# Attention on one Trainium2 core: products with V in groups of 3, 3, 3, 3, 2, 2 key tiles, a fixed order of one head, PSUM banks chosen by a count, nine P tiles, gate columns summed earlier

## The chip, the cores and the metric

The kernel runs on one core of one Trainium2 chip. The metric is the time of one execution on the device in microseconds (us). The engines of the core are named as the profile names them: PE (TensorE, with PEld for its weight loads), DVE (VectorE), ACT (ScalarE), POOL (GpSimd) and SP (SyncE, which issues DMAs). Each engine takes its instructions in program order. A difference of 0.2% is about what a measurement of this kernel can tell from none.

## The reference

A block with two halves, both gated by a condition vector `c`: attention with 16 heads of width 28 over 2048 rows of 448, and a gated MLP that mixes over rows. What the change touches is the first half and the six modulation vectors:

```
mod = (_silu(c) @ w_mod).reshape(c.shape[0], 6, 1, -1)
sa, ca, ga, sb, cb, gb = (mod[:, 0], mod[:, 1], mod[:, 2], mod[:, 3], mod[:, 4], mod[:, 5])
h = _layernorm(x, axis=-1) * (1 + ca) + sa
x = x + ga * _A_ref(h, A_wqkv, A_wo)
h = _layernorm(x, axis=-1) * (1 + cb) + sb
x = x + gb * _B_ref(h, B_w_in, B_w_sp, B_b_sp, B_w_out)
```

`_A_ref` is softmax attention: `q k^T / sqrt(28)`, softmax over the keys, times `v`, times `wo`. All of it is in float32.

## The kernel before

Every order is written out by hand: each engine runs its instructions as the program lists them, and an instruction waits only for the data or the buffer that it needs.

The attention stage runs head by head, in units `u` of one head and one tile of 128 keys (16 units a head, 256 in all). Unit `u` has four score products (`s_mm`, L649, out `st_ps`: 128 keys by 512 queries), each followed by an exponential on ACT (L653) into a P tile; and one product with V (`pv_mm`, L664, out `o_ps`), which is four matmuls on 32-column strips of the array, one for each block of 512 queries. These accumulate over the 16 key tiles of a head in one PSUM bank. The softmax needs a row maximum ahead of it. So the kernel also computes, 20 units earlier (`LEAD`), the transposed scores (`m_mm`, L584, out `mt`), and DVE reduces each to a column of maxima (L589, out `pm`). A head therefore has 64 score products, 64 products for the maxima and 16 products with V. At the end of a head's maxima, `m_max` (three short DVE steps, `mxv` and `mx`) and `m_fin` (a transpose on PE into `mtp`, a copy on DVE into `nf`, two DMAs from `nf` into two rows of `qst`) put the maxima where the next head's score products subtract them. `nf` is a single buffer. `n_copy` (L673, out `osb`) takes a finished `o_ps` off PSUM, and `n_sum`, `n_recip`, `n_bcast`, `n_mul` and `n_scatter` divide it by the sum of its P.

The order of the steady loop: unit after unit, `s m s m s m s m`, and behind every second unit the products with V of the two units before it, a group of 2 key tiles. PSUM has eight banks: three in turn for the scores (tag `s`), four in turn for the maxima (tag `m`), one for `o_ps`. A product into a bank waits until the reader of the bank's last content is done. P tiles (one holds 128 by 1024) come from a pool of six, which is three units.

All other work hangs on the units as events: loads of the next head, 80 sums of weight blocks for the second half (`ws_load`, `ws_add` on POOL, `ws_store`), and the gates. `mod_late` multiplies a tile of `w_late` by the silu row on POOL and sums it in halves into a column; `mod_end` adds one or turns the column into a row (`to_row`: a transpose into `mtp`, a copy into the same `nf`, a DMA from it). Sixteen of them are spread 10 units apart, in the order ga, sb, cb, gb. `wo_prep` scales and splits the output weight by `ga` at units 124 to 148, and `wout_prep` the last weight by `gb` at units 199 to 235.

Of the kernel before, what the change touches and what calls it, by code (L numbers as in the profile page):

```python
# [8 lines left out]
F32 = mybir.dt.float32  # L9
F32R = mybir.dt.float32r  # L10
AF = mybir.ActivationFunctionType
ALU = mybir.AluOpType
# [21 lines left out]
def tile_adaln_mha_gmlp(ctx, tc, x, wqkv, wo, w_in, w_spT, b_sp, w_out, cT, w_mod, w_late, out):  # L34
# [129 lines left out]
    def bank(name, kind=None):  # L164

        if kind is None:
            kind = "smsmsmm"[turn[0] % 7]
            turn[0] += 1
        return ring.tile([128, 512], F32, name=name, tag=kind, bufs=3 if kind == "s" else 4)

    def load_mod_chunk(c, eng):
# [390 lines left out]


    ppool = att.enter_context(tc.tile_pool(name="ppool", bufs=6))

    class Slots:

# [4 lines left out]
            return heapD[n][p, o : o + c.stop - c.start]  # L572

    OT = Slots()
    wos = hview(heapD[2], 0, 8, D)

    pms = {}

    steady = []

    def m_mm(j, kb):
        h, t = divmod(j, NT)
        mt = bank("mt", *steady)
        pe.matmul(  # L584
            mt, qst[h % 3][:, t * 128 : (t + 1) * 128], kst[h % 3][:, kb * 512 : (kb + 1) * 512], start=True, stop=True
        )
        if h not in pms:
            pms[h] = npool.tile([128, NT, 4], F32, name="pm")
        dve.tensor_reduce(out=pms[h][:, t, kb : kb + 1], in_=mt, axis=AX.X, op=ALU.max)  # L589

    mxs = {}

    def m_max(h):
        nm = npool.tile([128, NT], F32, name="mxv")
        dve.tensor_reduce(out=nm, in_=pms.pop(h), axis=AX.X, op=ALU.max, negate=True)
        mxs[h] = npool.tile([128, 2 * NT], F32R, name="mx2")
        dve.tensor_copy(mxs[h][:, 0:NT], nm)
        sub(dve, mxs[h][:, NT : 2 * NT], nm, mxs[h][:, 0:NT])

    def m_fin(h):  # L600
        mx = mxs.pop(h)
        tp = bank("mtp", *steady)
        pe.transpose(tp[0 : 2 * NT, 0:128], mx.bitcast(F32), ident)
# [5 lines left out]
    LATE = ("ga", "sb", "cb", "gb")  # L609
    gcols = {"sb": cols["sb"], "cb": cols["cb"], "ga": cols["sa"], "gb": cols["ca"]}  # L610
    mods = {}

    def silu_row():
        sp.dma_start(bcs["gb"], row(0))

    def mod_load(i):
        mods[i] = stage2.tile([128, D], F32, name="w_late", tag="ql")
# [2 lines left out]
    def mod_late(i):  # L620
        m, n = mods.pop(i), D // 2

        def add(dst, a, b):
            pool.tensor_tensor(out=dst, in0=a, in1=b, op=ALU.add)

        pool.tensor_tensor(out=m, in0=m, in1=bcs["gb"], op=ALU.mult)
        while n >= 7:
            add(m[:, 0:n], m[:, 0:n], m[:, n : 2 * n])
            n //= 2
        add(m[:, 0:3], m[:, 0:3], m[:, 3:6])  # L630
        add(m[:, 0:1], m[:, 0:1], m[:, 1:2])
        add(m[:, 2:3], m[:, 2:3], m[:, 6:7])
        add(gcols[LATE[i // 4]][:, i % 4 : i % 4 + 1], m[:, 0:1], m[:, 2:3])

    def mod_end(nm):
        if nm == "cb":
            pool.tensor_scalar(out=cols[nm], in0=cols[nm], scalar1=1.0, scalar2=None, op0=ALU.add)
        elif nm != "sb":
            to_row(gcols[nm], 1, *steady)

    def mod_row(nm):
        sp.dma_start(bcs[nm], row(1))
# [2 lines left out]

    def s_mm(u, qb):
        h, kt = divmod(u, NT)
        st = bank("st_ps", "s" if u + LEAD < NU else None)
        pe.matmul(st, kst[h % 3][:, kt * 128 : (kt + 1) * 128], qst[h % 3][:, qb * 512 : (qb + 1) * 512], start=True, stop=True)  # L649
# [3 lines left out]
        act.activation(p, st, AF.Exp, scale=SCALE)  # L653
        ptiles[u, qb] = p
# [2 lines left out]
    osb = {}  # L657

    def pv_mm(u):
        h, kt = divmod(u, NT)  # L660
        if kt == 0:
            otile[h] = ps_o.tile([128, 512], F32, name="o_ps", tag="o")
        for qb in range(4):
            pe.matmul(  # L664
                otile[h][32 * qb : 32 * qb + 32, :], V[:, kt, h, :], ptiles.pop((u, qb)), start=kt == 0, stop=kt == NT - 1
            )

    rts = {}

    def n_copy(h):  # L670
        osb[h] = stage.tile([128, 512], F32, name="osb", tag="qf")
        if h < H - 1:
            dve.tensor_copy(osb[h], otile.pop(h))  # L673
        else:
            act.activation(osb[h], otile.pop(h), AF.Copy)
# [55 lines left out]

    def wo_prep(i):
        pool.tensor_tensor(out=wo_raw[i], in0=wo_raw[i], in1=bcs["ga"], op=ALU.mult)
        weight_part(wos, i, wo_raw.pop(i), pool, pool)

    wout_t = {}

# [58 lines left out]

    LEAD = 20
    NU = H * NT
    events, late = {}, {}

    def at(slot, fn, *a, when=events):
# [2 lines left out]
    for h in range(H):  # L804
        if h >= 2:
            at(h * NT - LEAD - 10, load_head, h)
        e0 = (h + 1) * NT
        at(e0 + 1, n_copy, h)
# [5 lines left out]
        at(h * NT + NT - LEAD, m_max, h)  # L814
        at(max(h * NT + NT - LEAD, -2), m_fin, h, when=late)
    for c, hl in ((0, 4), (1, 9), (2, 13)):
        for qb in range(4):
            at((hl + 1) * NT + (12 + qb if c == 2 else 18 + 2 * qb), o_split, c, qb)
# [3 lines left out]
        at(slot + 5, ws_store, i)  # L822
    at(4, silu_row)
    for i in range(16):
        at(8 + 10 * i, mod_load, i)
        at(12 + 10 * i, mod_late, i)
    for i, nm in enumerate(LATE):
        at(46 + 40 * i, mod_end, nm, when=late)
        if nm in bcs:
            at(49 + 40 * i, mod_row, nm)  # L830
    for i in range(4):
        at(120 + 8 * i, wo_load, i)
        at(124 + 8 * i, wo_prep, i)
        at(200 + 8 * i, win_first, i)
    for f in range(7):
        at(196 + 6 * f, wout_raw, f)
        at(199 + 6 * f, wout_prep, f)
        at(201 + 6 * f, wout_store, f)

    load_head(1)  # L840

# [20 lines left out]
    steady.append("m")  # L862
    for u in range(NU + 1):
        for fn, a in events.pop(u, []):
            fn(*a)
        j = u + LEAD
        for qb in range(4 if u < NU else 0):
            s_mm(u, qb)
            if j < NU:
                m_mm(j, qb)  # L870
        if u % 2 == 0 and u > 0:
            pv_mm(u - 2)
            pv_mm(u - 1)
        for fn, a in late.pop(u, []):
            fn(*a)
    tail_events = {fn.__name__: [(fn, a)] for k in sorted(events) for fn, a in events[k]}

    def run_tail(*names):
# [5 lines left out]


    att.close()

    fh = ctx.enter_context(tc.tile_pool(name="fh", bufs=1))
    heapA = fh.tile([128, 8 * 896], F32R, name="heapA")
# [12 lines left out]
    def wo_mm(t, steps):  # L902
        if t not in wo_ps:
            wo_ps[t] = bank("wo_ps") if t % 8 < 7 else ps_o.tile([128, 512], F32, name="wo_ps", tag="o")
        for a, b in steps:
            pe.matmul(  # L906
                wo_ps[t][:, :D],
                OT[:, a, t * 128 : (t + 1) * 128],
                wos[:, b, :],
                start=(a, b) == STEPS[0],  # L910
                stop=(a, b) == STEPS[-1],
            )
# [539 lines left out]
```

## Time and profile before

| | |
|---|---|
| median of 3 runs | 1398.41 us (1398.05 to 1398.46) |
| the profiled execution | 1399.65 us |
| its span, first to last instruction | 1397.8 us |
| granted TensorE clock in it | 1.000 |
| DVE busy in the span | 1012.1 us (72%) |
| ACT busy in the span | 774.8 us (55%) |
| POOL busy in the span | 351.3 us (25%) |
| first and last score product | 147.1 and 864.0 us |

The page puts PE at 100% busy, yet matmuls are pipelined and each record lasts longer than the distance to the next one: a product of 512 columns has a record of 0.39 us, and the next begins 0.23 us after it. So PE's time is read from the starts of its matmuls, not from its busy share. For DVE and ACT the busy share can be read directly.

The attention stage takes half of the span, from 147 to 868 us. The other stages before and behind it have the same code in both kernels.

### The profile page before, as it was taken

The numbers are of one execution on the slowest core, as the hardware profiler recorded it, in microseconds if no ns is written. First come the engines' busy times: TensorE is split into PE (matmuls) and PEld (weight loads), VectorE is DVE, ScalarE is ACT, GpSimd is POOL, SyncE is SP. The second block draws the span as 40 slices with busy tenths as digits, with TensorE's granted clock in tenths as the row PEclk, the third lists the DMA queues.
The fourth block names the chain that finished last, engine by engine and source line by source line (L and its number), as shares of the span: only waits on it lengthen the run. The fifth ranks groups of instructions, "written<-read, shape, count | busy, mean of one in ns | idle before, by whom it ended". The sixth has DMA issues, their size and how long they took to land.

```text
span 1397.8 us, 20319 instructions
## 1 busy us (share of the span) xinstructions
PE 1391.5 (100%) x7187; PEld 989.6 (71%) x7187; DVE 1012.1 (72%) x1738; ACT 774.8 (55%) x1491; POOL 351.3 (25%) x452
## 2 busy tenths in 40 slices
PE   9999999999999999999999999999999999999998
PEld 8888655555555555555555555988998888888888
DVE  7588888888888888888888851750366655667473
ACT  5623677777766666767777778363234544334110
POOL 2043315332435254423221231000142430000000
PEclk9999999999999999999999999999999999999999
DMA  7364744666565556655334212434103333446353
GB/s 224 111 193 150 204 116 158 176 181 171 163 178 173 172 172 190 176 165 158 112 94 115 61 51 72 163 120 140 46 11 103 113 113 107 144 140 214 134 176 105
DMA packets 104406, 194.59 MB, mean 139 GB/s; under 512 B 17302, under 2 KB 34718, under 8 KB 101758
## 3 DMA queue, kind: packets, MB, share of 16 engines
q1 hardware_dynamic: 101874, 189.45, 44.7%
q10 hardware_dynamic: 2430, 3.84, 0.7%
q8 instruction: 56, 0.92, 0.3%
q14 instruction: 46, 0.38, 0.1%
HBM read 134.78 MB, written 53.67 MB: 135 GB/s over the span
## 4 chain that ended last, share of the span: by engine, by line
PE 98%; DVE 1%; ACT 0%; issue 0%; POOL 0%; POOLq 0%
PE st_ps L649 18%; PE o_ps L664 17%; PE mt L584 17%; PE acc L1224 6%; PE acc L1225 6%; PE acc L1226 6%; PE z_ps L1150 5%; PE z_ps L1036 5%; PE pq L288 5%; PE wo_ps L906 3%; PE pv L273 2%; PE y_ps L1326 2%; PE y_ps L1325 2%; PE y_ps L1327 2%; PE tp L118 1%; PE wu L237 1%
## 5 line engine op out<-in xcount | busy, mean ns | idle before, releaser
L589 DVE TENSOR_REDUCE pm<-mt 128x1 f32<-128x512 f32 x1024 | 631.1, 680 | 82.6 <-PE mt L584 82.2
L653 ACT ACTIVATE P<-st_ps 128x512 f32<-128x512 f32 x1024 | 514.6, 632 | 205.6 <-PE st_ps L649 205.6
L649 PE MATMUL st_ps<-qst,kst 128*128 128x512 f32 x1024 | 404.3, 406 | 0.2 <-DVE qf L294 0.2
L584 PE MATMUL mt<-kst,qst 128*128 128x512 f32 x1024 | 403.4, 394 | 0.1
L649 PEld LDWEIGHTS st_ps<-qst,kst 128*128 128x128 f32 x1024 | 191.3, 188 | 136.0 <-issue 92.2
L664 PE MATMUL o_ps<-P,V 128*32 128x512 f32 x2048 | 247.1, 598 | 0.0
L584 PEld LDWEIGHTS mt<-kst,qst 128*128 128x128 f32 x1024 | 192.4, 188 | 37.7 <-DVE pm L589 5.3
L792 POOL TENSOR_TENSOR ws_raw<-ws_raw 128x512 f32<-128x512 f32 x80 | 103.2, 1290 | 287.0 <-DMA ws_raw<-in_w_spT_dram 280.7
L1112 ACT ACTIVATE wsp_h<-raw_sp 128x512 fp32r<-128x512 f32 x112 | 70.2, 632 | 163.0 <-PE acc L1226 120.3
L85 DVE TENSOR_TENSOR wsp_l<-raw_sp,wsp_h 128x512 fp32r<-128x512 f32 x112 | 80.5, 729 | 90.8 <-ACT wsp_h L1112 90.1
L664 PEld LDWEIGHTS o_ps<-P,V 128*32 128x32 f32 x2048 | 54.7, 109 | 122.6 <-issue 114.9
L1224 PE MATMUL acc<-wsp_h,heapA 128*128 128x512 f32 x224 | 87.4, 390 | 0.1
L1225 PE MATMUL acc<-wsp_l,heapA 128*128 128x512 f32 x224 | 87.2, 389 | 0.0
L1226 PE MATMUL acc<-wsp_h,heapA 128*128 128x512 f32 x224 | 87.2, 389 | 0.0
L1226 PE MATMUL acc<-wsp_h,heapB 128*128 128x512 f32 x174 | 67.7, 389 | 0.0
L1225 PE MATMUL acc<-wsp_l,heapB 128*128 128x512 f32 x174 | 67.7, 389 | 0.0
L1224 PE MATMUL acc<-wsp_h,heapB 128*128 128x512 f32 x174 | 67.7, 389 | 0.0
L288 PE MATMUL pq<-heapD,heapD 128*128 128x512 f32 x196 | 62.1, 390 | 0.0
L1154 DVE BATCH_NORM_STATS2 stz<-z 128x6 f32<-128x448 f32 x32 | 19.9, 625 | 50.4 <-ACT z L1153 29.8
L1224 PEld LDWEIGHTS acc<-wsp_h,heapA 128*128 128x128 f32 x224 | 42.0, 188 | 9.4 <-DVE cD L1230 0.9
L1226 PEld LDWEIGHTS acc<-wsp_h,heapA 128*128 128x128 f32 x224 | 42.1, 188 | 8.8
L1225 PEld LDWEIGHTS acc<-wsp_l,heapA 128*128 128x128 f32 x224 | 42.1, 188 | 8.5
(223 smaller groups left out, 1646.3 us busy)
## 6 DMA issues: line engine op xcount, KB each, us to landing
ws_raw<-in_w_spT_dram SPq DMA_DIRECT2D x160, 256.0 KB
ws_scr<-ws_raw SPq DMA_DIRECT2D x80, 256.0 KB
raw_sp<-ws_scr SPq DMA_DIRECT2D x80, 256.0 KB
kst<-qk_scr SPq DMA_DIRECT2D x45, 224.0 KB
qst<-qk_scr SPq DMA_DIRECT2D x45, 224.0 KB
raw_sp<-in_w_spT_dram SPq DMA_DIRECT2D x32, 256.0 KB
qk_scr<-qh SPq DMA_DIRECT2D x28, 256.0 KB
qk_scr<-ql SPq DMA_DIRECT2D x28, 256.0 KB
```

The source lines that it names most:

```text
L85: eng.tensor_tensor(out=dst, in0=a, in1=hi.bitcast(F32), op=ALU.subtract)
L288: pe.matmul(pq, wqk[:, b, m * 128 : (m + 1) * 128], hT[g][:, a, :], start=j == 0, stop=j == NST - 1)
L584: pe.matmul(mt, qst[h % 3][:, t * 128 : (t + 1) * 128], kst[h % 3][:, kb * 512 : (kb + 1) * 512], start=True, stop=True)
L589: dve.tensor_reduce(out=pms[h][:, t, kb : kb + 1], in_=mt, axis=AX.X, op=ALU.max)
L649: pe.matmul(st, kst[h % 3][:, kt * 128 : (kt + 1) * 128], qst[h % 3][:, qb * 512 : (qb + 1) * 512], start=True, stop=True)
L653: act.activation(p, st, AF.Exp, scale=SCALE)
L664: pe.matmul(otile[h][32 * qb : 32 * qb + 32, :], V[:, kt, h, :], ptiles.pop((u, qb)), start=kt == 0, stop=kt == NT - 1)
L792: pool.tensor_tensor(out=a, in0=a, in1=b, op=SUMS[i // 16][2])
L1112: act.activation(hi, raw, AF.Copy)
L1224: pe.matmul(acc[i], zh, hi, start=st == 0, stop=False)
L1225: pe.matmul(acc[i], zh, lo, start=False, stop=False)
L1226: pe.matmul(acc[i], zl, hi, start=False, stop=st == 7)
```

## The change

1. For heads 0 to 13 the loop over units is replaced by a string of 137 letters that is run once for each head (`ORDER`). `s` is a score product, `m` a product for the maxima, a digit a group of products with V of so many key tiles (3, 3, 3, 3, 2, 2 from the head's second group on, the first 2 being the last two key tiles of the head before), `C` the copy `n_copy` of the head before, `X` and `F` the steps `m_max` and `m_fin` for the next head. The first `2` of head 0 has nothing to multiply and is left out. Heads 14 and 15 keep the loop of before.
2. In the whole attention stage a product's bank is named by `Queue`: the program counts, while it is written out, when each of seven banks should come free, and takes the first. So a bank serves scores and maxima alike, and PE waits for just the bank that the count named. `o_ps` keeps its own bank. The PSUM pools are closed and opened anew at the start and at the end of the stage.
3. P tiles: nine in turn instead of six for heads 0 to 13. The three more lie in the memory in which before lay the prepared `wo`.
4. The gates are summed in the order gb, sb, cb, ga, 6 units apart instead of 10. `wout` is loaded, scaled and stored at units 120 to 173 instead of 196 to 237; `wo` is loaded and scaled at units 228 to 246 instead of 120 to 148, when the three P tiles are no longer needed.

```
-        st = bank("st_ps", "s" if u + LEAD < NU else None)
+        st = bank("st_ps", queue.bank("s"))
...
-            ptiles[u, -1] = ppool.tile([128, 2, 512], F32, name="P")
+            ptiles[u, -1] = p_tile(u, qb // 2)
...
+    p_more = dpool.tile([128, 4 * 896], F32, name="p_more", tag="heapD2")
+
+    def p_tile(u, half):
+        i = (2 * u + half) % 9 - 6
+        if u >= GROUPED * NT or i < 0:
+            return ppool.tile([128, 2, 512], F32, name="P")
+        return p_more[:, i * 1024 : (i + 1) * 1024].rearrange("p (a b) -> p a b", b=512)
...
+        MM, TURN, PV, PV_IN, PV_OUT = 230.5, 110, 860, 113, 100
+        LAG = {"s": 300, "m": 200, "F": 200, "C": 200}
+        TIMES = {"s": (480, 178), "m": (602, 137), "F": (310, 137), "C": (610, 0), "X": (680, 0)}
...
+        def work(self, kind, start):
+            eng = "act" if kind == "s" else "dve"
+            self.late[eng] = max(self.late[eng], start) + self.TIMES[kind][0]
+            return self.late[eng] + self.TIMES[kind][1]
...
+            b = min(range(7), key=lambda i: self.free[i])
+            start = max(self.pe, self.free[b])
+            if kind == "F":
+                self.pe = start + self.TURN
+            else:
+                self.pe = start + self.MM + (104 if self.after_pv else 0)
+                self.after_pv = 0
+            self.free[b] = self.work(kind, self.pe + self.LAG[kind])
+            return b
...
+    GROUPED = H - 2
+    ORDER = (
+        "ssmsmsmm2Csmsmssmmssmmssssmmm3smsmsmsmssmmssssmmmmm3smsmssmsmsmmssmm"
+        "smsmsmssmmsm3smsmsmsmsssmmsmmssmmXm3Fmsmssmmsmssmsmsmms2smsmsmssmssmm"
+    )
...
+            elif k in "23" and (h or over or n["s"] > 4 * int(k)):
+                for u in range(over, over + int(k)):
+                    pv_mm(u)
+                over += int(k)
+                for e in [e for e in sorted(late) if e <= over]:
+                    for fn, a in late.pop(e):
+                        fn(*a)
...
-        at(8 + 10 * i, mod_load, i)
-        at(12 + 10 * i, mod_late, i)
+        at(8 + 6 * i, mod_load, i)
+        at(12 + 6 * i, mod_late, i)
```

Three places show how this moves instructions. First PE, in the middle of a steady head: before, one stretch between two groups of products with V (an `o_ps` row of 8 matmuls is two key tiles).

```order
L649 MATMUL st_ps<-qst_840,kst_839 128x512
L584 MATMUL mt<-kst_841,qst_842 128x512
L664 MATMUL o_ps<-P,V 32x512 x8
L649 MATMUL st_ps<-qst_840,kst_839 128x512
L584 MATMUL mt<-kst_841,qst_842 128x512
```

Now, the stretch that ends with the second group of three (12 matmuls, whose P lie in both memories):

```order
L697 MATMUL st_ps<-qst_844,kst_843 128x512 x2
L631 MATMUL mt<-kst_839,qst_840 128x512 x2
L697 MATMUL st_ps<-qst_844,kst_843 128x512 x4
L631 MATMUL mt<-kst_839,qst_840 128x512 x5
L713 MATMUL o_ps<-p_more,V 32x512 x4
L713 MATMUL o_ps<-P,V 32x512 x8
L697 MATMUL st_ps<-qst_844,kst_843 128x512
L631 MATMUL mt<-kst_839,qst_840 128x512
```

The score products are no longer one for one with the products for the maxima: four scores and then five `mt` stand ahead of the group, so five banks hold work for DVE when it begins.

Second DVE, where a gate's column is turned into a row. `nf` of 4x128 is that gate's copy, `nf` of 32x128 the copy of `m_fin`; both write the one `nf` buffer. Before, for the first of the two gates that come by this way:

```order
L589 TENSOR_REDUCE pm<-mt 128x1 [waits PE_49] x4
L605 COPY nf<-mtp 32x128 [waits DMAHW7_49,PE_49]
L589 TENSOR_REDUCE pm<-mt 128x1 [waits PE_49] x8
L556 COPY nf<-mtp 4x128 [waits DMAHW5_49,DMAHW4_49,PE_49]
L589 TENSOR_REDUCE pm<-mt 128x1 [waits PE_49] x8
```

Now, for the last gate, `ga`:

```order
L85 TENSOR_TENSOR mx_5371<-mxv,mx_5371 128x16 [waits DVE_49]
L636 TENSOR_REDUCE pm<-mt 128x1 [waits PE_49]
L558 COPY nf<-mtp 4x128 [waits DMAHW3_49,PE_49]
L653 COPY nf<-mtp 32x128 [waits DMAHW2_49,DVE_49,PE_49]
L636 TENSOR_REDUCE pm<-mt 128x1 [waits PE_49] x19
```

The two copies now stand next to each other, and the second waits for the DMA that reads the first one's `nf`; eight reductions lay between them before.

Third PE, where the attention stage begins, behind the last projection (`pq`). Before:

```order
L584 MATMUL mt<-kst_841,qst_842 128x512 [waits DVE_49]
L288 MATMUL pq<-heapD_90,heapF 128x512
L649 MATMUL st_ps<-qst_840,kst_839 128x512 [waits DMAHW3_49,DMAHW2_49]
L584 MATMUL mt<-kst_841,qst_842 128x512 [waits Activation_49]
L649 MATMUL st_ps<-qst_840,kst_839 128x512 [waits DVE_49]
```

Now:

```order
L290 MATMUL pq<-heapD_90,heapF 128x512
L697 MATMUL st_ps<-qst_840,kst_839 128x512 [waits DMAHW2_49,DMAHW3_49,DVE_49,Activation_49]
L697 MATMUL st_ps<-qst_840,kst_839 128x512
L631 MATMUL mt<-kst_841,qst_842 128x512
L697 MATMUL st_ps<-qst_840,kst_839 128x512
```

The first score product now waits for DVE and ACT to be done with the banks of the old pool; the ones behind it wait for nothing.

More of the change, by code (lines that the diff above doesn't have):

```diff
@@ L574, in tile_adaln_mha_gmlp @@
     OT = Slots()
[L575 removed]
+    wos = []
     pms = {}
[L579 removed]
+    named = []
     def m_mm(j, kb):
         h, t = divmod(j, NT)
[L583 removed]
+        mt = bank("mt", queue.bank("m") if named else None)
         pe.matmul(
@@ L593, in m_max @@
     def m_max(h):
+        queue.other("X")
         nm = npool.tile([128, NT], F32, name="mxv")
@@ L601, in m_fin @@
         mx = mxs.pop(h)
-        tp = bank("mtp", *steady)
+        tp = bank("mtp", queue.bank("F") if named else None)
         pe.transpose(tp[0 : 2 * NT, 0:128], mx.bitcast(F32), ident)
@@ L638, in mod_end @@
         elif nm != "sb":
-            to_row(gcols[nm], 1, *steady)
+            to_row(gcols[nm], 1, queue.bank("F"))
     def mod_row(nm):
@@ L670, in n_copy @@
     def n_copy(h):
+        queue.other("C")
         osb[h] = stage.tile([128, 512], F32, name="osb", tag="qf")
```

84 lines of the change are left out of this document (66 added, 18 removed).

## The prediction, made before the changed kernel ran

> **What bounds the kernel now.** I read the page's chain first, then sums over stretches, then the timeline of single products.
>
> ```profile
> span 1397.8 us, 20319 instructions
> PE 98%; DVE 1%; ACT 0%; issue 0%; POOL 0%; POOLq 0%
> 376.10:790.30 414.20, 414.20 (x2313) 239.25 (x2313) 364.72 (x631) 289.41 (x576) 146.81 (x200) 1.00 0.52 150
> ```
>
> 98% of the chain that ended last is PE's. The third row is a stretch of nine steady heads, 46.02 us each; the copy behind "m_fin" shows the same step between heads 8 and 9 (`mtp` starts at 460.18 and 506.19 in the rows below, 46.01 apart). Its columns are PE, PEld, DVE, ACT, POOL. So a head has 40.52 us of DVE work (364.72 / 9) and 5.50 us of idle DVE, and ACT is idle for 13.9 us. Now one group of products with V:
>
> ```profile
> 457.77 0.40 PE L649 MATMUL st_ps<-qst,kst 128*128 128x512 f32 x1
> 458.00 0.40 PE L584 MATMUL mt<-kst,qst 128*128 128x512 f32 x1
> 458.33 1.92 PE L664 MATMUL o_ps<-P,V 128*32 128x512 f32 x16
> 460.18 0.29 PE L603 MATMUL mtp<-ident,mx 128*32 128x128 f32 x1
> ...
> 506.19 0.28 PE L603 MATMUL mtp<-ident,mx 128*32 128x128 f32 x1
> ...
> 458.79 0.13 PEld L664 LDWEIGHTS o_ps<-P,V 128*32 128x32 f32 x4 [0.30 <-issue]
> 459.21 0.13 PEld L664 LDWEIGHTS o_ps<-P,V 128*32 128x32 f32 x4 [0.30 <-issue]
> ...
> 500.43 0.50 PE L649 MATMUL st_ps<-qst,kst 128*128 128x512 f32 x1
> 500.76 0.39 PE L584 MATMUL mt<-kst,qst 128*128 128x512 f32 x1
> ```
>
> Plain products start 0.23 us apart (457.77, 458.00). Into the group it is 0.33, so 0.10 more. From the first matmul of the group to the next product it is 1.85. Each set of four strips takes about 0.43 (458.79 to 459.21 gives 0.42), two sets make a key tile, 0.86, and two key tiles 1.72; 0.13 is left for the way out. The product behind a group (500.43) takes 0.33 to the next, 0.10 more. **A group costs 0.10 + 0.13 + 0.10 = 0.33 to 0.34 us beside its products.** The head: 128 x 0.231 + 16 x 0.859 + 8 x 0.339 = 29.57 + 13.74 + 2.71 = 46.02 us. That is the measured head: PE never waits for long, and DVE has 5.5 us to spare. The waits view says the same of the banks:
>
> ```profile
> PEld mt L584 <- DVE pm L589: 5.3, 24, 0.5
> ```
>
> In the whole span the weight loads of the 1024 products `mt` wait for a reduction 24 times, 5.3 us in all.
>
> **The groups.** The 222 key tiles of the fixed order come in 83 groups where 111 stood before. 28 x 0.339 = **9.5 us less** on the engine that sets the end. Without waits a head takes 45.34 us, and then DVE's idle time must shrink from 5.50 to 4.8.
>
> **The waits.** That is the doubtful part: during a group of three PE makes nothing new for DVE for 3.48 us (2.58 for the products, 0.13 out, 0.34 for the score product behind it, 0.43 until its reduction can start), and DVE lives on what the banks hold. How fast are the banks turned over, and what does a late one cost?
>
> ```profile
> 554.82 1.27 DVE L589 TENSOR_REDUCE pm<-mt 128x1 f32<-128x512 f32 x2
> ...
> 501.19 2.48 DVE L589 TENSOR_REDUCE pm<-mt 128x1 f32<-128x512 f32 x4 [0.86 <-PE mt L584]
> ...
> 500.96 4.03 ACT L653 ACTIVATE P<-st_ps 128x512 f32<-128x512 f32 x8 [1.72 <-PE st_ps L649]
> ...
> 555.28 0.40 PE L649 MATMUL st_ps<-qst,kst 128*128 128x512 f32 x1
> 555.54 0.50 PE L584 MATMUL mt<-kst,qst 128*128 128x512 f32 x1
> 555.87 0.40 PE L649 MATMUL st_ps<-qst,kst 128*128 128x512 f32 x1
> 556.14 0.50 PE L584 MATMUL mt<-kst,qst 128*128 128x512 f32 x1
> 556.56 0.63 PE L664 MATMUL o_ps<-P,V 128*32 128x512 f32 x3
> ...
> 555.54 0.19 PEld L584 LDWEIGHTS mt<-kst,qst 128*128 128x128 f32 x1 [0.30 <-DVE pm L589]
> ...
> 556.13 0.19 PEld L584 LDWEIGHTS mt<-kst,qst 128*128 128x128 f32 x1 [0.30 <-DVE pm L589]
> ...
> 471.88 0.69 DVE L673 COPY osb<-o_ps 128x512 f32<-128x512 f32 x1 [0.31 <-issue]
> ```
>
> Two reductions take 1.27 and four 2.48: 0.60 apart, 0.68 long. A reduction starts 0.43 behind its product (500.76, 501.19), an exponential 0.5 behind its score (500.43, 500.96), and eight exponentials in 4.03 are 0.49 apart. The late bank: the second reduction of the first row ends at 556.09, and the weight load that waited for it starts at 556.13. From 555.28 to 555.87, two steps, PE takes 0.59 where 0.46 is plain; the product into the late bank starts with its load, and the step behind it is 0.33 instead of 0.23. So a late load costs what it is late, **and 0.10 us more, because its weights aren't loaded beside the product before.** A bank of a reduction that runs in a queue is ready for a product 0.68 + 0.04 + 0.10 = 0.83 us after the reduction's start. The count in the change takes 602 + 137 = 739 ns.
>
> The Trainium skill states the other thing ("TensorE: Matmul & The Clock Gate", section on the array of 32x32 sub-arrays): a matmul can begin before its weight load has completed. By that rule a late bank would cost no 0.10; the step at 555.54 speaks against it, and what it would give stands among the rivals.
>
> I walked the 137 letters of a steady head with these lengths, "n_copy" at 1.0 us (0.69 and the 0.31 of issue), and each product into the bank that the count names. The same walk of the old order has no waits, as the trace. In the new order PE waits: 0.09 us ahead of the first 2; 0.25 in the stretch that ends in five `mt`; 0.35 in the stretch of 28 products; 0.09 ahead of the last 3; 0.08 behind `F`; 0.01 and 0.02 elsewhere. **0.89 us a head.** The second account agrees. DVE's work left when a group begins, by the walk, is 1.58, 2.19, 2.11 and 2.86 us for the threes and 1.60 for the 2, so DVE idles 3.48 - 1.58 = 1.90, then 1.29, 1.37, 0.28 (the copy of `F` comes early there) and, with 2.61 for a 2, 1.01, in sum 5.85; with 40.4 of work that is a head of 46.25. So 45.34 + 0.89 = 46.23 to 46.25: what the groups save, 14 x 0.68 = 9.5, the waits take, 14 x 0.89 = 12.5. **Net 3.0 us more**, less 0.3 for the odd waits of before. The ends are 0 (no waits) and, with one miss of a whole reduction more in each head, 0.89 + 0.60.
>
> **The start.** The first score product now waits for DVE and ACT to have left the old banks.
>
> ```profile
> 147.13 0.39 PE L649 MATMUL st_ps<-qst,kst 128*128 128x512 f32 x1
> ...
> 148.45 0.50 PE L649 MATMUL st_ps<-qst,kst 128*128 128x512 f32 x1 [0.25 <-DVE qf L294]
> ...
> 147.72 0.68 DVE L294 COPY qf<-pq 128x512 f32<-128x512 f32 x1
> ```
>
> The copy `qf` ends at 148.40. Until then PE made four products; now the first comes at 148.45, and the four, 0.92 us, come later: **0.9 us**, between 0 (DVE catches up) and 1.4.
>
> **The two copies into nf.** The second copy holds DVE until the gate's DMA has read the first.
>
> ```profile
> 629.82 0.33 SPq L557 DMA_DIRECT2D m_scr<-nf  x1
> ...
> 627.94 0.28 DVE L556 COPY nf<-mtp 4x128 f32<-4x128 f32 x1 [0.43 <-PE mtp L554]
> ...
> L679 SPq DMA_DIRECT2D rt<-osb x15: 621/632/643, 196.7 to 836.8; - x15
> L683 DVE RECIPROCAL rt<-rt x15: 240/243/252, 204.7 to 838.7; 128x16 f32<-128x16 f32 x15
> ```
>
> Before, that DMA was issued 1.6 us after the copy's end (628.22, 629.82), behind other DMAs on SP. A DMA of this size takes 1.9 us to be used (836.8 to 838.7, the last of each). So DVE stands for 2.2 to 3.5 us once, all reductions behind it queue, and PE stops when the banks are full. Of that the next groups' idle time gives some back: **2 us**, between 0 and 3.5.
>
> **At nothing.** Nine P tiles: at most seven are held when a group begins, so no exponential waits for one; the cover is two tiles, and without it ACT has 13.9 us idle a head. A second wait on some 280 exponentials is hidden there too. The moved gates and weights: POOL is busy for 146.81 of 414.20 us and SP's DMAs keep their distance of two or three units, 5.8 to 8.6 us, from what uses them. `wout`'s loads and stores now stand on SP's queue among those of `m_fin` in other heads, `wo`'s loads among those near the end; `m_fin`'s rows are needed 31 products and a group of 2 behind `F`, 31 x 0.231 + 2.06 = 9.2 us, which is what hides a queue there. If that cover goes, each microsecond late is one of PE's. ACT's and DVE's last instructions and the pool at the end: below 0.5.
>
> **Sum.** -9.5 + 12.5 - 0.3 + 0.9 + 2.0 = +5.6. On the profiled execution, 1399.65 (span 1397.8), that is 1405.2; its median is 1.24 lower, so **1404.0**.
>
> **Rivals.**
> A late bank without the 0.10 (the rule quoted above): the same walk gives 0.43 of waits, a head of 45.78, 14 x (0.43 - 0.68) = -3.5, and with the one-time terms 1397.5. For it: nothing but that single late loads are few in this trace. Against it: 555.54 to 555.87. 20%.
> The order leaves no waits at all: DVE idles only 4.8 us a head. -9.5 + 2.9 gives 1391.8. This is the faster side; it decides where five or more reductions stand when a three begins. Against it: seven banks, of which scores hold some. 13%.
> Misses: a bank comes free in another order than counted, and PE stands before a busy one with a free one beside it. One a head, 0.60 x 14 = 8.4, gives 1412; it decides where "n_copy", counted at 0.61 and 1.0 in its row, shifts the rest. 12%.
> That the groups aren't fewer is excluded by the order of instructions.
>
> **How the numbers follow.** My forecast, 1404.0, has 55%, from 1400 to 1408 by the one-time terms (0 to 4.9) and 0.1 us a head. The range of 8 in 10 leaves out half of the miss (6), most of the case without waits (10) and the forecast's far ends (4): 1393.5 to 1409. About 0.2%, 2.8 us, is what a measurement can tell from no change: slower means over 1401.2, with 80% of the forecast's 55 (44) and 10 of the miss, 54; same has 15 of the case without the 0.10 and 9 of the forecast's lower end, 24; faster has the case without waits, 13, and the rest of those two and of the miss, 9, in sum 22.
>
> **What would show it.** The windows of nine heads: 46.2 a head, DVE idle 5.8. Waits of `mt`'s weight loads for `pm` at about 12 us in all where they were 5.3, most in the third and fourth stretch. One DVE wait of 2 to 3.5 us at the `nf` of 32x128 in head 6. A head of 45.8 or below would show the waits wrong, and one above 46.6 the count of banks.

## The result, and the profile after

| | before | changed kernel |
|---|---|---|
| median | 1398.43 us (4 runs, 1398.05 to 1398.72) | 1407.45 us (4 runs, 1406.67 to 1408.28) |
| ratio to before | | 1.0067, 95% interval 1.0055 to 1.0078 |
| profiled execution (span) | 1399.65 (1397.8) us | 1406.67 (1404.8) us |

The change costs 0.67%. The forecast was 1404.0, slower, with a range of 1393.5 to 1409. The two profiled executions are 7.0 us apart; the forecast's sum for them was 5.6.

The page of the changed kernel, first the span and the chain of waits:

```profile
span 1404.8 us, 20647 instructions
PE 95%; DVE 3%; issue 0%; DMA 0%; ACT 0%; POOL 0%; SPq 0%; DVEq 0%; POOLq 0%; ACTq 0%
```

Before, PE had 98% of the chain and DVE 1%. Now DVE has 3%: a part of what sets the end has gone back to DVE.

The length of a steady head is read best from the transpose of `m_fin`, of which there is one a head. Its first and last start in a window from 480 to 800 us, in the profile of before and then of the changed kernel (seven transposes, so six heads):

```profile
L603 PE MATMUL mtp<-ident,mx x7: 284/284/285, 506.2 to 782.8; 128*32 128x128 f32 x7
```

```profile
L651 PE MATMUL mtp<-ident,mx x7: 283/284/284, 509.8 to 788.3; 128*32 128x128 f32 x7
```

(782.8 - 506.2) / 6 = 46.10 us, and (788.3 - 509.8) / 6 = 46.42 us. The forecast for the changed kernel was 46.23 to 46.25. (Three of the six heads of before hold an odd wait, 46.2 to 46.3 us each; the other three take 45.98 to 46.00.) The busy time of PE, PEld, DVE, ACT and POOL over the same six heads of the changed kernel:

```profile
509.80:788.30 278.50, 278.33 (x1547) 158.25 (x1544) 242.71 (x421) 192.10 (x384) 66.56 (x59) 1.00 0.49 140
```

DVE is idle for (278.50 - 242.71) / 6 = 5.97 us a head, where the forecast said 5.85. Without waits it would have been 4.8.

The waits of PE's weight loads, from the view of waits of the changed kernel:

```profile
PEld st_ps L697 <- DVE pm L636: 50.6, 75, 0.8
...
PEld st_ps L697 <- issue: 25.1, 29, 1.6
...
PEld mt L631 <- DVE pm L636: 9.8, 43, 0.5
...
PEld st_ps L697 <- ACT P L701: 7.2, 38, 0.3
...
PEld mt L631 <- ACT P L701: 6.6, 37, 0.2
```

Two traps in reading it. Most of the 50.6 us are not lost: behind a group the next load stands idle for 0.7 to 0.9 us on average (50.6 / 75, 25.1 / 29) while PE still multiplies, and that idle time is put down to whatever semaphore came last (the stage has 100 groups, and behind 14 of them the transpose comes first). In half_both, a run shown below in which almost no bank is late, nearly the same idle time is there, 70.9 us for 50.6 + 25.1, and is put down to no wait at all:

```profile
PEld st_ps L699 <- issue: 70.9, 84, 1.3
```

And since a bank now serves both kinds, a product `mt` waits for ACT as often as for DVE. So the sum of one row was a poor thing to forecast; the heads' length wasn't.

### The profile page after: what moved, and what is told of

It reads as the page before. It is cut to its first block, busy times and chain, and to the rows that moved or that the text cites. A ratio compares the mean times of both kernels' runs of the same rounds, so it can differ in the third digit from the quotient of the medians.

```text
span 1404.8 us, 20647 instructions
## 1 busy us (share of the span) xinstructions
PE 1396.0 (99%) x7187; PEld 984.8 (70%) x7187; DVE 1011.5 (72%) x1738; ACT 772.3 (55%) x1491; POOL 353.6 (25%) x452
## 4 chain that ended last, share of the span: by engine, by line
PE 95%; DVE 3%; issue 0%; DMA 0%; ACT 0%; POOL 0%; SPq 0%; DVEq 0%; POOLq 0%; ACTq 0%
PE st_ps L697 18%; PE mt L631 17%; PE o_ps L713 16%; PE acc L1318 6%; PE acc L1320 6%; PE acc L1319 6%; PE z_ps L1244 5%; PE z_ps L1130 5%; PE pq L290 5%; PE pv L275 2%; PE y_ps L1420 2%; PE y_ps L1421 2%; PE y_ps L1419 2%; PE wo_ps L1000 1%; DVE pm L636 1%; PE tp L118 1%
## 5 line engine op out<-in xcount | busy, mean ns | idle before, releaser
L701 ACT ACTIVATE P<-st_ps 128x512 f32<-128x512 f32 x728 | 370.2, 643 | 143.6 <-PE st_ps L697 143.6
L631 PE MATMUL mt<-kst,qst 128*128 128x512 f32 x1024 | 370.5, 404 | 0.6 <-DVE nf L653 0.5
L697 PE MATMUL st_ps<-qst,kst 128*128 128x512 f32 x1024 | 358.1, 405 | 1.3 <-issue 1.2
L697 PEld LDWEIGHTS st_ps<-qst,kst 128*128 128x128 f32 x1024 | 188.5, 187 | 122.0 <-DVE pm L636 50.6
L631 PEld LDWEIGHTS mt<-kst,qst 128*128 128x128 f32 x1024 | 189.1, 188 | 65.1 <-DVE pm L636 9.8
L713 PE MATMUL o_ps<-P,V 128*32 128x512 f32 x1456 | 200.3, 597 | 0.0
L701 ACT ACTIVATE p_more<-st_ps 128x512 f32<-128x512 f32 x296 | 155.0, 639 | 72.4 <-PE st_ps L697 72.4
L713 PEld LDWEIGHTS o_ps<-P,V 128*32 128x32 f32 x1456 | 46.3, 109 | 86.7 <-issue 81.3
L713 PE MATMUL o_ps<-p_more,V 128*32 128x512 f32 x592 | 97.7, 597 | 0.0
L1318 PEld LDWEIGHTS acc<-wsp_h,heapA 128*128 128x128 f32 x224 | 42.0, 188 | 9.4 <-DVE cD L1324 0.9
```

Of the source, the lines that this page charges most:

```text
L631: pe.matmul(mt, qst[h % 3][:, t * 128 : (t + 1) * 128], kst[h % 3][:, kb * 512 : (kb + 1) * 512], start=True, stop=True)
L713: pe.matmul(otile[h][32 * qb : 32 * qb + 32, :], V[:, kt, h, :], ptiles.pop((u, qb)), start=kt == 0, stop=kt == NT - 1)
L1318: pe.matmul(acc[i], zh, hi, start=st == 0, stop=False)
```

## The experiments

The twelve runs below were all timed in five rounds against the kernel before. Heads are worked out as above, from the first and last of seven transposes (six in seven_groups).

| run | groups a head | us a head | median, us | ratio to before (95%) |
|---|---|---|---|---|
| changed kernel | 6 | 46.42 | 1407.45 | 1.0055 to 1.0078 |
| half_reduce | 6 | 45.90 | 1398.84 | 0.9995 to 1.0014 |
| half_both | 6 | 45.08 | 1387.09 | 0.9913 to 0.9941 |
| half_both_twos | 8 | 45.97 | 1397.47 | 0.9984 to 1.0002 |
| twos | 8 | 46.05 | 1399.87 | 1.0000 to 1.0018 |
| nf_apart | 6 | 46.40 | 1406.07 | 1.0041 to 1.0066 |
| crossing_behind | 6 | 46.62 | 1409.01 | 1.0059 to 1.0087 |
| six_found | 6 | 46.53 | 1407.47 | 1.0051 to 1.0076 |
| seven_groups | 7 | 48.9 | 1436.68 | 1.0255 to 1.0283 |
| seven_mended | 7 | 46.20 | 1401.38 | 1.0012 to 1.0030 |
| seven_old_count | 7 | 46.17 | 1401.79 | 1.0015 to 1.0034 |
| walk_order | 7 | 46.63 | 1407.07 | 1.0054 to 1.0080 |
| walk_copy | 7 | 45.75 | 1396.14 | 0.9979 to 0.9997 |

### Are the banks the cause? half_reduce, half_both, half_both_twos

```
-        dve.tensor_reduce(out=pms[h][:, t, kb : kb + 1], in_=mt, axis=AX.X, op=ALU.max)
+        dve.tensor_reduce(out=pms[h][:, t, kb : kb + 1], in_=mt[:, 0:256], axis=AX.X, op=ALU.max)
```

> The changed kernel, with each reduction for the maxima taken over 256 of the 512 columns (half of the keys are left out of the maxima, and the exponent is multiplied by an eighth of the scale so that it stays finite). DVE's reductions get shorter, about 0.33 us apart instead of 0.60; PE's instructions stay the same. Theory (PE waits for banks, and the banks wait for DVE): the waits go that stand ahead of the groups; those for banks of scores stay. A walk of the order gives 45.87 us a head where 46.39 was measured, so 14 x -0.52 = -7.3, and less of the stall at nf: 1399, between 1396 and 1401. Rival (the groups of three themselves cost PE more than 0.34 us and 0.86 a key tile): the head stays at 46.3 to 46.4 and the time at 1406 to 1407.

Measured: 45.90 us a head and 1398.84 us, both as the theory had them. PE's instructions are untouched, so 0.52 us a head of the changed kernel goes with the length of the reductions. What is left stands at ACT, as the waits view of half_reduce shows; among its 60 largest rows none has a load of `mt` or `st_ps` that waits for a reduction any more:

```profile
PEld mt L631 <- ACT P L701: 21.8, 118, 0.3
PEld st_ps L697 <- ACT P L701: 17.5, 90, 0.3
```

So the exponentials were halved as well (the lines that put the P tiles into one block of memory and fill it with ones are left out here):

```
-        act.activation(p, st, AF.Exp, scale=SCALE)
+        act.activation(p[:, 0:256], st[:, 0:256], AF.Exp, scale=SCALE * 0.125)
```

> half_reduce with the exponentials halved too: each takes 256 of the 512 queries (the other half of P holds ones from nine fills at the start of the stage, so half of the attention is left out; half of the keys are left out of the maxima). PE's instructions are those of the changed kernel. Theory (a head of six groups takes PE 45.34 us, and all above it is waiting for DVE's and ACT's banks): the wait that half_reduce still had for scores goes, 45.34 to 45.5 us a head, six groups at 0.34 each as predicted; 14 x -0.45 from half_reduce and 1 to 2 us for the fills: 1394, between 1391.5 and 1396.5. Rival (groups of three cost more than 0.34 each): 45.9 us a head as in half_reduce, 1399 or more.

Measured: 1387.09 us, better than the theory's range. The head, from half_both's transposes:

```profile
L653 PE MATMUL mtp<-ident,mx x7: 283/284/284, 497.9 to 768.4; 128*32 128x128 f32 x7
```

(768.4 - 497.9) / 6 = 45.08 us. This is what PE needs for a head of six groups when no bank is late: of the loads of `mt` and `st_ps`, the waits view of half_both has only three that wait for a reduction or an exponential. It is 0.26 less than the 45.34 of the count. The timeline of half_both shows a stretch up to a group and the way out:

```profile
530.23 0.39 PE L699 MATMUL st_ps<-qst,kst 128*128 128x512 f32 x1
530.46 0.39 PE L633 MATMUL mt<-kst,qst 128*128 128x512 f32 x1
530.68 0.39 PE L699 MATMUL st_ps<-qst,kst 128*128 128x512 f32 x1
530.91 0.39 PE L633 MATMUL mt<-kst,qst 128*128 128x512 f32 x1
531.14 0.62 PE L699 MATMUL st_ps<-qst,kst 128*128 128x512 f32 x2
531.59 0.62 PE L633 MATMUL mt<-kst,qst 128*128 128x512 f32 x2
532.04 0.39 PE L699 MATMUL st_ps<-qst,kst 128*128 128x512 f32 x1
532.27 0.39 PE L633 MATMUL mt<-kst,qst 128*128 128x512 f32 x1
532.59 1.06 PE L715 MATMUL o_ps<-p_more,V 128*32 128x512 f32 x8
...
535.30 0.50 PE L699 MATMUL st_ps<-qst,kst 128*128 128x512 f32 x1
535.63 0.39 PE L633 MATMUL mt<-kst,qst 128*128 128x512 f32 x1
...
537.94 0.61 PE L633 MATMUL mt<-kst,qst 128*128 128x512 f32 x2
...
539.53 0.84 PE L633 MATMUL mt<-kst,qst 128*128 128x512 f32 x3
```

Nine steps from 530.23 to 532.27 take 2.04 us, 0.227 each (0.231 in the forecast), and the step into the group 0.32 (0.33). The group of three and its way out take 535.30 - 532.59 = 2.71, and the product behind it 0.33: 0.859 x 3 and 0.13, as counted. The step is another matter. The ten steps from 535.63 to 537.94, close behind the group, are 0.231 each, the seven from there to 539.53 again 0.227.

The last of the three puts the order of twos under the same shortened reductions and exponentials, so that only the groups differ:

> half_both (half of the keys out of the maxima, half of the queries out of the exponentials) with the order of twos: eight groups of 2 a head in place of six. With no bank late in either, the two differ by the groups alone. Theory (a group costs 0.33 to 0.34 us beside its products): 45.08 + 2 x 0.33 = 45.75 us a head, 14 x 0.67 = 9.4 and less of the stall at nf (1.2): 1395.3, between 1394 and 1397; and the head of before, 46.10, then holds 0.35 us of its own that its banks cost it. Rival (a group of three costs more than one of two, so that fewer groups save less): under 45.5 us a head, 1392 or less.

```profile
L653 PE MATMUL mtp<-ident,mx x7: 284/284/284, 505.5 to 781.3; 128*32 128x128 f32 x7
```

And its timeline from the end of a group of 2 to the next:

```profile
534.26 0.50 PE L699 MATMUL st_ps<-qst,kst 128*128 128x512 f32 x1
534.61 0.40 PE L633 MATMUL mt<-kst,qst 128*128 128x512 f32 x1
...
536.93 0.39 PE L633 MATMUL mt<-kst,qst 128*128 128x512 f32 x1
...
537.84 0.39 PE L633 MATMUL mt<-kst,qst 128*128 128x512 f32 x1
538.16 0.64 PE L715 MATMUL o_ps<-p_more,V 128*32 128x512 f32 x4
```

Measured: (781.3 - 505.5) / 6 = 45.97 us a head, 1397.47 us. Two groups fewer are worth 45.97 - 45.08 = 0.89 us, not 0.67, and the time lies just above the theory's range. The rows show where the other 0.22 is. Here too the ten steps close behind a group (534.61 to 536.93, a group of 2) take 0.232 each and the four behind them 0.228, although score and maximum products alternate all the way. So a group has one more cost, which the forecast had as part of a plain step of 0.231: about 10 x 0.005 = 0.05 us in the steps behind it. And behind a group of three the first product and the ten steps take 0.33 + 2.31, behind a group of 2 they take 0.35 + 2.32, 0.03 more. Estimated from these rows over steps of 0.227, a group of 2 costs 0.09 on the way in, 0.13 out, 0.12 in the first product and 0.05 behind it, in sum 0.39, and a group of three 0.36. Eight groups of 2 against two of 2 and four of three then make 8 x 0.39 - 2 x 0.39 - 4 x 0.36 = 0.90. Why the first steps behind a group are longer stays open. The rival, that longer groups cost more, falls.

So the account of a head is: the groups save 0.89; waiting, meant as all that goes when the reductions and exponentials are shortened, was 46.10 - 45.97 = 0.13 before and is 46.42 - 45.08 = 1.34 now, 1.21 more. 1.21 - 0.89 = 0.32, the difference measured.

### Is it the order alone? twos, nf_apart

```
-        "ssmsmsmm2Csmsmssmmssmmssssmmm3smsmsmsmssmmssssmmmmm3smsmssmsmsmmssmm"
-        "smsmsmssmmsm3smsmsmsmsssmmsmmssmmXm3Fmsmssmmsmssmsmsmms2smsmsmssmssmm"
+        "smsmsmsm2Csmsmsmsmsmsmsmsm2smsmsmsmsmsmsmsm2smsmsmsmsmsmsmsm2smsmsmsm"
+        "smsmsmsm2smsmsmsmsmsmsmsm2smsmsmsmXsmsmsmsm2Fsmsmsmsmsmsmsmsm2smsmsmsm"
```

> The changed kernel with the order of before (score and maximum product in turn, groups of 2 only, the copies and the maxima at their places of before), all else as changed: banks by the count, nine P tiles, gates and weights moved, pools opened anew. Theory (only the order costs time): head 46.02 to 46.04 us, no two copies into nf next to each other, the later start of 0.8 us stays: before's time plus 1, 1399.4, between 1398.5 and 1400.5. Rival (banks by a count, or the moved gates and weights, cost time as well): over 1401.5, with waits of PE for banks or DMAs between the groups.

Measured: 46.05 us a head and 1399.87 us. Banks by a count, nine P tiles, the moved gates and weights and the pools opened anew cost 0.0 to 0.2% together (1.4 us by the medians, of which the forecast had 0.9 for the pools). The forecast's "at nothing" holds within that.

```
-        nf = npool.tile([2 * NT, 128], F32, name="nf", bufs=1)
+        nf = npool.tile([2 * NT, 128], F32, name="nf_max", bufs=1)
```

This stands in `m_fin` alone; the gate's copy keeps `nf`.

> The changed kernel with a buffer of its own for the copy of m_fin, so that it does not wait for the gate's DMA out of nf. Theory: the head in which the two copies meet takes 46.4 us like its neighbours instead of 47.9, so -1.5 us: 1406.0, between 1405.4 and 1406.6. Rival (that head is long because the DMA of m_fin itself, or the gate's row, comes late): the head stays at 47.5 or more and the time at 1407.4.

Measured: 1406.07, 1.4 us less. That is less than the 0.2% that times can tell, so it rests on the head: the transposes of `m_fin` at its ends are 461.98 and 509.75 in the changed kernel, 47.8 us apart, and 463.03 and 509.44 here, 46.4. What it removes, in the timeline of DVE and of SP's DMA issues of the changed kernel:

```profile
462.18 0.28 DVE L558 COPY nf<-mtp 4x128 f32<-4x128 f32 x1 [0.23 <-PE mtp L556]
463.77 0.28 DVE L653 COPY nf<-mtp 32x128 f32<-32x128 f32 x1 [1.31 <-PE mt L631]
463.98 5.45 DVE L636 TENSOR_REDUCE pm<-mt 128x1 f32<-128x512 f32 x9
```

```profile
462.49 0.27 SPq L559 DMA_DIRECT2D m_scr<-nf  x1
464.08 1.20 SPq L655 DMA_DIRECT2D qst<-nf  x2
```

The gate's copy ends at 462.46, its DMA is issued at 462.49, and the copy of `m_fin` starts at 463.77: 1.31 us of idle DVE. The row names a product `mt` as the releaser, which had long been done; the DMA is what the instruction waited for.

### The first product of a new head: crossing_behind

A steady head of the changed kernel has 1.03 us over plain steps of 0.231 and its groups' 0.34. Of that, 0.28 stands in the stretch ahead of the last group of three, where the forecast had 0.09. The rows there in the timeline, of the loads, and the group of semaphore instructions of PE's sequencer at that place:

```profile
552.26 0.50 PEld L631 LDWEIGHTS mt<-kst,qst 128*128 128x128 f32 x2
552.97 0.19 PEld L631 LDWEIGHTS mt<-kst,qst 128*128 128x128 f32 x1 [0.21 <-ACT p_more L701]
```

```profile
L631 PEldq EVENT_SEMAPHORE  x4: 51/51/51, 552.6 to 552.9; - x4
```

The last `mt` ahead of the group is the first of a new head, and waits for seven DMA queues and a bank. All had come (the exponentials named in the row end at 552.70); still four semaphore instructions start at 552.6 to 552.9, about 0.1 us apart, and the load follows at 552.97, 0.4 after the load before it (552.58, the second of the first row), and PE loses some 0.17 by it. Before, the same four stood in the middle of a stretch and cost nothing:

```profile
L584 PEldq EVENT_SEMAPHORE  x4: 51/51/51, 548.3 to 548.6; - x4
```

There no late bank stood just ahead, and the four were over in time. The next kernel moves that one product behind the group:

```
-        ...smsmsmsmsssmmsmmssmmXm3Fmsmssmm...
+        ...smsmsmsmsssmmsmmssmmX3mFmsmssmm...
```

> The changed kernel with one product moved: the first maximum product of the head after next, which waits for seven DMA queues in four semaphore steps 0.106 us apart, stands first behind the third group of three instead of last ahead of it. Theory (it is the turnover of the banks that sets the head, and DVE has one reduction less queued when that group begins): the 0.17 us of the steps go, and the products before the group of 2 wait that much longer, 46.40 us a head: the time stays, 1407.3, between 1406.3 and 1408.3. Rival (the steps add to all else): 14 x -0.17 = -2.3, 1405.1.

Measured: 46.62 us a head, 1409.01 us. The steps' 0.17 went from that stretch (0.11 is left of 0.28); the stretch behind it (19 products up to the group of 2), which had no wait in the changed kernel, now has 0.3 in six of seven heads and 0.9 in one. The rival, a gain of 2.3 us, falls. The theory had the direction, not the size: by the heads more comes back than was saved, while the two times are too close to be told apart. Why the waiting moves (by the theory, since DVE has one reduction less queued during the group) was not tried by itself.

### What does a late load cost? six_found

```
...
+        "ssmsmmsmsmssm2sCsmsmsmsmsmmsmsmsmmmm3smsmsmssmsmsmmsmsssss3msmsmssms"
+        "msmsmmmsmmsmm3msmsmssmsmssmmsmssmXmss2Fsmsmssmsmssmmmsmmssmm3smsmsmsm"
```

> Six groups a head (2, 3, 3, 3, 2, 3), in the order that the walk finds best when a late bank costs only its lateness, that is without the 0.10 us of the weight load and without the four semaphore steps. Banks named by the walk's count, nf apart. Theory (a late load costs 0.10 us more): the walk with these costs gives 46.05 us a head, 14 x -0.34 and -1.4 from the changed kernel: 1401.3, between 1399 and 1403.5. Rival (a product begins before its load is done, so that only the lateness counts): 45.45 us a head, 14 x -0.94 and -1.4: 1392.9, under 1395.

Measured: 46.53 us a head, 1407.47 us. If a late bank cost only its lateness, this order would give 45.45. It is worse than the theory's 46.05 too. The next part has a length that was missing: with it the walk gives 46.44 (see what was expected of walk_order), 0.39 more, and the rival is off by 1.1 us a head. The rival's walk was not redone with that length. The timeline of the changed kernel, matmuls and loads of the stretch of 28, shows what a late load does:

```profile
543.15 0.39 PE L697 MATMUL st_ps<-qst,kst 128*128 128x512 f32 x1
543.41 0.50 PE L631 MATMUL mt<-kst,qst 128*128 128x512 f32 x1
543.75 0.71 PE L697 MATMUL st_ps<-qst,kst 128*128 128x512 f32 x2
```

```profile
543.41 0.19 PEld L631 LDWEIGHTS mt<-kst,qst 128*128 128x128 f32 x1 [0.24 <-DVE pm L636]
543.52 0.19 PEld L697 LDWEIGHTS st_ps<-qst,kst 128*128 128x128 f32 x1
```

The product is recorded from the start of its late load, 0.26 behind the one before, and the next one starts 0.34 later: 0.60 for two steps of 0.23. 0.14 is lost, of which the lateness is 0.03 and the load 0.11. So the rule of the Trainium skill that stands among the rivals ("TensorE: Matmul & The Clock Gate", section on the array of 32x32 sub-arrays), by which a matmul can begin before its load has completed, gives no saving that these rows show.

### Can an order beat both? seven_groups, seven_mended, seven_old_count, walk_order, walk_copy

In the walk, orders of seven groups a head have next to no waits. The first runs below each found a length that the walk lacked.

> The changed kernel with an order of 7 groups a head (2, 3, 3, 2, 1, 3, 2) found by a walk that counts 0.83 us from the start of a reduction to the next product in its bank, 0.10 us of it the weight load, and the four semaphore steps ahead of the first product of a new head; banks named by that same count; nf apart as well. Theory: the walk has next to no waits, 45.74 us a head, 14 x -0.65 = -9.1 and -1.5 for nf: 1396.8, between 1395 and 1398.5, faster than before by 0.1%. Rival (the 0.10 us is not the reason, or fewer groups always bring as much waiting as they save): 46.0 us a head or more, 1400 or more.

Measured: 48.9 us a head, 1436.68 us. The order has `F` two letters behind `X`; the walk let the transpose start when its bank was free, but it needs `m_max`, which stands behind all of DVE's queue:

```profile
PE mtp L661 <- DVE mx L85: 29.2, 14, 3.0
```

14 times, 29.2 us, 2.1 each, of the 3.1 us by which a head is longer than the walk's 45.74; the rest was not followed up. (In this order the row of the last gate is read from DRAM ahead of the point where it is written, so `ga` holds the values of `gb`; the times are those of the same instructions.)

> Seven groups a head again (2, 3, 2, 1, 3, 3, 2), in an order found by the walk with one rule more: the transpose of m_fin waits for m_max, for which DVE first works off its queue, so the two stand 4 products apart; the row of a gate is read 8 units later. Bank names by the walk's count, nf apart. Theory: next to no waits, 45.72 us a head, 14 x -0.67 = -9.4 and -1.4 for nf from the changed kernel: 1396.2, between 1394.5 and 1398, faster than before by 0.15%. Rival (fewer groups always bring as much waiting as they save): 46.0 us a head or more, 1399.5 or more.

> The same order of seven groups as in seven_mended, with the banks named by the change's own count (739 ns from a reduction's start, the copy n_copy at 610 ns, no load of weights). Theory (names matter where the count has n_copy too short): the walk with these names has one more wait of 0.24 us a head, at a product behind the copy, 45.95 us a head: 3.2 us more than seven_mended. Rival (PE takes any order of the names alike): the same time as seven_mended within 1 us.

Measured: 46.20 and 46.17 us a head, 1401.38 and 1401.79 us: both times stand where their rivals had them. The heads are 0.48 above the walk's 45.72 and 0.22 above its 45.95. Two lengths came out of these traces. The reader of the first product behind a group starts 0.10 later than that of another product (a reduction 0.53 behind its product instead of 0.43), just as that product itself takes 0.10 more to the next. And in seven_mended's own count the copy stood 0.3 us late, as the order has a score product between group and copy. By the walk both kernels therefore name a wrong bank at one place of a head, and the comparison of the two counts can't tell whether names matter; no run shows these places.

> Seven groups a head (2, 2, 3, 2, 2, 2, 3) with the change's own bank count, found by the walk with one more length: the reader of the first product behind a group starts 0.10 us later than that of another product. That length puts the walk at 46.47 us for the changed kernel (46.39 measured), 46.54 for crossing_behind (46.53), 46.26 for seven_mended (46.12), 46.44 for six_found (46.53) and 46.04 for twos (46.0). Theory: 45.82 us a head, 14 x -0.2 from twos: 1397, between 1395.5 and 1398.5, which is faster than before by 0.1%, less than the measurement can tell. Rival (the walk still lacks a wait of the size of a group's saving, 0.34): 46.1 us a head, 1401.

Measured: 46.63 us a head, 1407.07 us, beyond the rival too. In 13 heads the group that begins a head stands still, as the timeline and the waits view of walk_order show:

```profile
525.98 0.68 DVE L723 COPY osb<-o_ps 128x512 f32<-128x512 f32 x1
...
526.80 1.06 PE L713 MATMUL o_ps<-P,V 128*32 128x512 f32 x8 [0.51 <-DVE osb L723]
```

```profile
PE o_ps L713 <- DVE osb L723: 6.9, 13, 0.6
```

`o_ps` has one bank; the order has the copy late, in DVE's queue, and the next head's first group waits for its end, 526.66. That is 0.5 of the 0.8 us by which a head is longer than the walk's.

> Seven groups a head (2, 3, 2, 2, 2, 2, 3) again, with the change's own bank count, nf apart, found by the walk with the wait that walk_order turned out to have: the first group of a new head stands until DVE has copied the old o_ps off its one bank, so the copy comes directly behind the last group of a head and 22 products before the next one. Theory (all waits of a size are now in the walk): 45.82 us a head, no group later than 0.1 us: 14 x -0.2 from twos, 1397, between 1395.5 and 1398.5. Rival (there is always another wait that a shorter head uncovers): 46.0 us a head or more, 1399.5 or more.

```
...
+        "mmsmssssmmsm2Csmsmssmsmmssssmsmm3smsmsmssmssmsmmmsmm2msmssmsmmsmsmssm"
+        "sm2smsmssmmsmssmmmssmm2msmsmssmsmsmmssXmsm2Fsmsmssmmsmsmmmmmss3smsmss"
```

```profile
L651 PE MATMUL mtp<-ident,mx x7: 284/284/285, 504.0 to 778.5; 128*32 128x128 f32 x7
```

Measured: (778.5 - 504.0) / 6 = 45.75 us a head (45.82 expected), 1396.14 us, ratio 0.9988 (0.9979 to 0.9997). This order takes 0.8% less than the changed kernel and 0.12% less than before. The second gain is below the 0.2% that a measurement can tell, and its interval only just leaves out none. By the head, 45.75 us where the eight groups of twos take 46.05, the rival falls: fewer groups need not bring as much waiting as they save.

## Why the prediction was right

**The groups, -9.5 us.** Right in mechanism, too small: half_both against half_both_twos gives 0.89 us a head, 14 x 0.89 = 12.5. The 0.34 of a group is confirmed by its rows. What the forecast lacked are the longer steps behind a group, which it had taken for the plain step of both orders, 0.231; away from a group the step is 0.227.

**The waits, +12.5 us.** Right in mechanism, and half_reduce and half_both show it: with DVE and ACT shortened they go. Their size is 1.34 us a head over that of half_both, 1.21 more than before, 14 x 1.21 = 16.9, where the forecast had 12.5 less 0.3 for before. Place by place in steady heads, worked out from the starts of the products and counted over plain steps of 0.231: 0.11 ahead of the first 2 (0.09 forecast), 0.21 in the stretch that ends in five `mt` (0.25), 0.39 in the stretch of 28 (0.35), 0.28 ahead of the last 3 (0.09), about 0 behind `F` (0.08). Four of five are within 0.08. (Against the same stretches of half_both the five are 0.14, 0.26, 0.47, 0.33 and 0.05, and so make up the 1.34 with 0.1 elsewhere; whether these last hundredths are waits for banks, the rows don't tell.) The fourth lacked the four semaphore steps of the first product of a new head; in that stretch they make 14 x 0.17 = 2.4 us, more than the whole 1.4 by which the sum for the profiled execution was short. The order of instructions had shown that product's seven DMA waits; the forecast took them for free, as they were before. Taking them out of the stretch did not shorten the kernel, as crossing_behind shows.

**The start, +0.9.** The first score product of the changed kernel:

```profile
148.16 0.70 PE L697 MATMUL st_ps<-qst,kst 128*128 128x512 f32 x2 [1.20 <-issue]
```

It was 147.13 before, so 1.0 later. No run took the wait at the pools away, so what it costs at the end is not shown.

**The copies into nf, +2.0.** The stall is there, once, in head 6. It took 1.31 us of DVE and about 1.4 us of the head: the DMA was issued 0.03 us behind the copy, not 1.6, with no DMA of SP's just ahead of it. The forecast's bounds were 0 and 3.5.

**At nothing.** Shown by twos, within 0.2%.

**The rivals.** A late bank without the 0.10: the rows of the changed kernel speak against it, and six_found, 1.1 us a head from what it gives. No waits at all: half_both shows what it would be worth, 45.08 us a head. Misses of the count: none in the changed kernel's own order is shown; one a head in seven_mended and seven_old_count follows from the walk alone.

**What would show it.** DVE's idle time came as said, 5.85 against 5.97, and the head, 46.42, lies between the two bounds that were set, 45.8 and 46.6. The wait at `nf` came, shorter (1.31 us for 2 to 3.5). The 12 us of `mt` waiting for `pm` did not come (9.8): with banks shared by both kinds the same lateness is spread over several rows.

Put together, -12.5 + 16.9 + 1.0 + 1.4 = 6.8 us, and 7.0 were measured. So the sum of the forecast was near, although its two large terms were too small by 3.0 and 4.7 us. Most of these two misses is one and the same: the forecast's head without waits, 45.34, is 0.26 above that of half_both, 3.6 us in 14 heads, and makes the saving and the waiting look smaller alike, so that it cancels. What is left of them, 1.7 us by which the forecast had the heads too cheap, was in part made up by the 0.6 by which it had `nf` too dear, and that is luck.

## What to carry to other kernels

When an engine that sets the end is made to do its other work in longer pieces, ask what the next engine in the chain lives on meanwhile, and count the turnover of the buffers between them to the last 0.1 us: here the weight load's 0.10 and the 0.10 of the first product behind a group moved a head by tenths. A saving on the bound engine and the waiting that it causes are best told apart by shortening the other engines' work, not by reading the waits view. A wait that is free in one order can cost time in another, 0.17 us a head here behind a late buffer; but moving it may only move the waiting, as crossing_behind shows.

## What the runs showed of the hardware that was not expected

- Four semaphore instructions ahead of one weight load, all of them long satisfied, stand 0.1 us apart and took 0.17 us of PE's time where the load before them was late (552.6 to 552.9 in the changed kernel), and nothing at the place of before (548.3 to 548.6).
- With no bank late, the ten steps close behind a group of products with V take 0.231 to 0.232 us each, and the ones behind them 0.227 to 0.228, in half_both and in half_both_twos alike, whatever the order of score and maximum products. Why stays open.
- A product directly behind a group hands its result on 0.10 us later than another: in seven_mended an idle DVE starts its reduction 0.53 behind it, not 0.43.
- A DMA of 2 KB out of SBUF let its buffer go at most 1.28 us after its issue (462.49 to 463.77, where the next copy into `nf` starts), less than the 1.9 that the forecast took from issue to use.
